# Chunk attention and two feed-forward layers on one core: another block order at the start of the first layer, and one list of single operations for 48 steps

## The chip, the cores and the metric

One NeuronCore of a Trainium2 chip. The metric is the device time of one execution in microseconds; 1665.48 us is the median of three runs of the kernel before.

## The reference

Attention within chunks of 64 positions on float32 q, k and v of shape (8, 8, 576, 64), then a feed-forward layer whose activation is a quotient of two polynomials, then one with the activation s * relu(h)^2 + b. Both layers have 4608 tokens, a model width of 512 and a hidden width of 2048.

```python
scores = scale * np.matmul(q_c, k_c.transpose(0, 1, 2, 4, 3))
scores = scores - np.max(scores, axis=-1, keepdims=True)
attn = np.exp(scores)
attn = attn / (np.sum(attn, axis=-1, keepdims=True) + 1e-09)
out = np.matmul(attn, v_c)
...
h = x @ w_in
P = a[0] + a[1] * h + a[2] * h2 + a[3] * h3
Q = 1.0 + np.abs(b[0]) * np.abs(h) + np.abs(b[1]) * h2
g = P / (Q + 1e-06)
return (g @ w_out).astype(np.float32)
...
h = x @ w_in
r = np.maximum(h, 0.0)
g = s * (r * r) + b
return (g @ w_out).astype(np.float32)
```

## The kernel before

**Tiles and steps.** The 4608 tokens are nine blocks of 512; the hidden width is sixteen slices of 128. A step is one block and one slice: a first product h = w_in x (`mm1`, token M, twelve matmuls of 128x128 by 512 columns), the activation (tokens B, t, r, p, b, l, E, N), a split of its result g into a high and a low part (H, y), and a second product into the block's four accumulators (`mm2`, token R, twelve matmuls). Every operand is held as a high and a low half in a reduced float format, hence three matmuls for each product. The first layer has 144 steps; the second begins in the same manner and goes on with a scheme of seven products for pairs of blocks (`finish`), whose work stays as it is.

**Banks.** h of step i lies in one of three PSUM banks, i modulo 3. The activation writes its exponential back into h and reads it last in `ew_d` (token N, three VectorE operations, the last at line 608). So `mm1` of step i waits for `ew_d` of step i-3.

**Weights.** A slice of w_in or w_out arrives as 512 KB of 64-bit words (token w, `w_stage`, into one of four buffers big0 to big3). ScalarE takes the words apart (f, two operations), VectorE clamps, shifts and joins them for two slices at once (g, lines 396, 400 and twice 403), GpSimd adds (c, line 406), ScalarE makes the high half (d) and GpSimd or VectorE the low half (G or D, line 417). There are 32 such tiles, numbered w0 to w31 in the order in which the steps come to need them.

**Attention.** It runs in 36 groups of 128 rows, four to a block. q and k of each of the first eight groups arrive in four transfers of 64 partitions (P, `att_load_rows`, line 194), which read a chunk of 64 positions from each of two batches; v comes in four (L). These groups use weight buffers of the second half of the slices that are still empty (tags w1_8 to w1_15 and w0_8 to w0_15). TensorE transposes q and k (T), ScalarE copies them out (q, k, line 270), TensorE forms scores (S), VectorE takes the maximum and subtracts it (s, two operations for each of two halves, lines 301 and 302), ScalarE exponentiates (e), VectorE sums and inverts (m, lines 313 to 315), GpSimd or VectorE normalises (n), TensorE transposes (A) and multiplies by v (V); ScalarE writes the high half of the block's x (v) and VectorE the low half (u, line 366). Later groups are turned by VectorE instead (X, line 277). Two buffers hold x of two blocks.

**Order.** Nothing is reordered: each engine runs its instructions in the order in which the program issues them, and the DMA queues of SP and of ACT stand in the order of these two engines' instructions. `START` is a string of tokens, a letter and a number each, that `play` turns into calls: it holds steps 0 to 32, except the tail of the last ones. Its operations are whole ones: g1P is four VectorE operations in a row. A loop of one fixed pattern follows for the steps up to 127, with the attention of later groups laid in by a table of times (`att_at`). The steps' blocks go 0, 1, 0, 1 with half of the slices each, then 2, 3 and on with all sixteen; the first halves' results of blocks 0 and 1 are stored to memory (`store`) and loaded and added (`part_load`, `add`) when the second halves end.

Of the kernel before, what the change touches and what calls it, by code (L numbers as in the profile page):

```python
# [59 lines left out]
)  # L60

BEGUN = 33

# [38 lines left out]
def tile_chunk_attention__then__rational_ffn__then__relu2_ffn(  # L102
# [80 lines left out]
    def heads(n):  # L183
        u, j = divmod(n, S // CH)
        return 2 * H * u, j * CH

    def att_load_rows(n, dma=SP):


        h0, s0 = heads(n)  # L190
# [1249 lines left out]
```

## Time and profile before

| what | value |
|---|---|
| median of three runs (1665.36 to 1665.6) | 1665.48 us |
| the profiled execution: its own time | 1667.5 us |
| the profiled execution: its span of instructions | 1665.4 us |
| PE (TensorE) busy | 1604.4 us, 96% |
| DVE (VectorE) busy | 1311.4 us, 79% |
| ACT (ScalarE) busy | 1091.3 us, 66% |
| POOL (GpSimd) busy | 678.1 us, 41% |

The busy shares are means over the whole span. The page also gives them in 40 slices of 41.6 us, as tenths (9 is 90% or more), with the granted clock of TensorE and the DMA engines' share:

```profile
PE   4689999999999999999999999899999999999997
...
DVE  5899988887788878788789867877457886788677
...
PEclk8899999999999999999999999999999999999999
DMA  9643224112231321313123242897577659666854
```

A reader looks at the left end: the first four or five slices differ from the rest on every row. A row of the timeline gives start and length in us, engine, line, operation, output and inputs, how many, and in square brackets how long the engine stood idle before it and what ended that. "Idle" in the text is a stretch's length less the engine's busy time in it.

### The profile page before, as it was taken

To read this page: it belongs to the slowest core of one execution; us is meant where nothing else is said; L and a number is where in the kernel's file an instruction comes from. 1 tells how busy PE (TensorE), PEld (TensorE's weight loads), DVE (VectorE), ACT (ScalarE), POOL (GpSimd) and SP (SyncE) were. 2 spreads that over 40 slices of the span, in tenths; PEclk is the share of its full clock that TensorE was granted. 3 is DMA by queue.
4 is the path that set the end of the run, shared out by engine and by line. 5 is a ranking of instruction groups with operands and counts; after the bars stand their busy time and mean duration, and the time that the engine had idled before them with its cause. 6 is when DMAs were issued, how large, how long until landed. Compare 5 with 4: busy or idle time off the path is not lost.

```text
span 1665.4 us, 26182 instructions
## 1 busy us (share of the span) xinstructions
PE 1604.4 (96%) x9148; PEld 1313.3 (79%) x9148; DVE 1311.4 (79%) x2071; ACT 1091.3 (66%) x1824; POOL 678.1 (41%) x576
## 2 busy tenths in 40 slices
PE   4689999999999999999999999899999999999997
PEld 3577777888888888888887888788888888888886
DVE  5899988887788878788789867877457886788677
ACT  5778765666666666666687777667565766576563
POOL 4678775666556655666577656210000000000000
PEclk8899999999999999999999999999999999999999
DMA  9643224112231321313123242897577659666854
GB/s 205 160 124 115 73 55 111 34 29 64 39 57 31 60 39 33 59 31 77 33 82 112 92 127 101 276 325 246 190 252 241 194 151 276 219 222 161 286 182 67
DMA packets 339971, 217.76 MB, mean 131 GB/s; under 512 B 262528, under 2 KB 297344, under 8 KB 339840
## 3 DMA queue, kind: packets, MB, share of 16 engines
q1 hardware_dynamic: 326320, 211.63, 44.2%
q10 hardware_dynamic: 13520, 4.46, 1.3%
q8 instruction: 72, 1.18, 0.3%
q14 instruction: 59, 0.48, 0.1%
HBM read 163.58 MB, written 52.43 MB: 130 GB/s over the span
## 4 chain that ended last, share of the span: by engine, by line
PE 85%; DVE 8%; ACT 2%; issue 2%; DMA 1%; POOL 1%; SPq 0%; DVEq 0%; ACTq 0%; POOLq 0%
PE acc L478 27%; PE ae L1041 12%; PE h L460 9%; PE h L461 9%; PE h L462 9%; PE hA L980 8%; PE hE L980 4%; PE hc L980 2%; PE hc L1041 2%; PE pat L350 1%; PE pat L289 1%; PE pat L325 1%; DVE h L607 1%; DVE t L608 1%; DVE ah L606 1%
## 5 line engine op out<-in xcount | busy, mean ns | idle before, releaser
L460 PE MATMUL h<-xh,w 128*128 128x512 f32 x768 | 308.6, 402 | 9.3 <-DVE t L608 5.2
L462 PE MATMUL h<-xh,w 128*128 128x512 f32 x768 | 301.7, 393 | 0.0
L461 PE MATMUL h<-xl,w 128*128 128x512 f32 x768 | 301.5, 393 | 0.0
L478 PE MATMUL acc<-gh,w 128*128 128x512 f32 x1152 | 285.5, 390 | 0.6 <-ACT gh L616 0.6
L478 PEld LDWEIGHTS acc<-gh,w 128*128 128x128 f32 x1152 | 215.7, 188 | 46.0 <-ACT gh L616 1.0
L1041 PE MATMUL ae<-gs,wo 128*128 128x512 f32 x864 | 219.4, 391 | 2.3 <-DVE acc L1062 1.2
L568 POOL TENSOR_SCALAR r<-ah,ab_sb 128x512 f32<-128x512 f32 x138 | 110.1, 798 | 235.4 <-ACT ah L551 235.1
L1041 PEld LDWEIGHTS ae<-gs,wo 128*128 128x128 f32 x864 | 161.8, 188 | 38.6 <-DVE acc L1062 2.4
L571 POOL TENSOR_TENSOR r<-r,ah 128x512 f32<-128x512 f32 x140 | 182.4, 1303 | 13.8 <-ACT r L566 2.2
L460 PEld LDWEIGHTS h<-xh,w 128*128 128x128 f32 x768 | 145.7, 190 | 43.2 <-DVE t L608 8.6
L622 POOL TENSOR_TENSOR gl<-t,gh 128x512 fp32r<-128x512 f32 x129 | 167.8, 1301 | 16.2 <-ACT gh L616 14.5
L462 PEld LDWEIGHTS h<-xh,w 128*128 128x128 f32 x768 | 145.3, 189 | 31.3
L461 PEld LDWEIGHTS h<-xl,w 128*128 128x128 f32 x768 | 145.8, 190 | 29.0 <-DVE xl L366 0.5
L606 DVE SCALAR_TENSOR_TENSOR ah<-r,h 128x512 f32<-128x512 f32 x144 | 98.3, 683 | 79.3 <-ACT h L599 78.7
L478 PE MATMUL acc<-gl,w 128*128 128x512 f32 x576 | 154.2, 390 | 0.0
L980 PE MATMUL hA<-xs,wi 128*128 128x512 f32 x576 | 146.7, 390 | 0.7 <-ACT g L991 0.7
L616 ACT ACTIVATE gh<-t 128x512 fp32r<-128x512 f32 x144 | 90.8, 631 | 78.0 <-DVE t L608 71.4
L406 POOL TENSOR_TENSOR w<-w,wst 128x512 int32<-128x512 int32 x64 | 94.6, 1487 | 79.2 <-DVE w L403 48.5
L980 PEld LDWEIGHTS hA<-xs,wi 128*128 128x128 f32 x576 | 108.0, 188 | 23.7 <-ACT g L991 1.1
L478 PEld LDWEIGHTS acc<-gl,w 128*128 128x128 f32 x576 | 108.1, 188 | 22.6 <-POOL gl L622 0.3
L599 ACT ACTIVATE h<-ah,exb 128x512 f32<-128x512 f32 x144 | 99.5, 691 | 39.1 <-DVE t L590 36.6
L594 ACT ACTIVATE ah<-r,lnb 128x512 f32<-128x512 f32 x144 | 103.4, 718 | 30.3 <-POOL r L571 29.8
(133 smaller groups left out, 3035.2 us busy)
## 6 DMA issues: line engine op xcount, KB each, us to landing
wi<-wq SPq DMA_DIRECT2D x84, 512.0 KB, 4.1
wo<-wq SPq DMA_DIRECT2D x84, 512.0 KB, 4.7
wq<-wo SPq DMA_DIRECT2D x64, 256.0 KB, 3.1
wst<-in_moe_w_out_dram SPq DMA_DIRECT2D x30, 512.0 KB, 4.6
wst<-in_moe_w_in_dram SPq DMA_DIRECT2D x29, 512.0 KB, 5.1
wq<-w SPq DMA_DIRECT2D x48, 256.0 KB, 3.6
qk<-in_q_dram SPq DMA_DIRECT2D x224, 32.0 KB, 2.1
qk<-in_k_dram SPq DMA_DIRECT2D x224, 32.0 KB, 2.1
```

The costliest lines, as they stand in the source:

```text
L460: T.matmul(h, wh, xh[:, kk], start=kk == 0, stop=False)
L461: T.matmul(h, wh, xl[:, kk], start=False, stop=False)
L462: T.matmul(h, wl, xh[:, kk], start=False, stop=kk == KD - 1)
L478: T.matmul(o, l, r, start=first and n == 0, stop=last and n == 2)
L568: eng.tensor_scalar(out=r, in0=ah, scalar1=ab_sb[:, 1:2], scalar2=ab_sb[:, 0:1], op0=ALU.mult, op1=ALU.add)
L571: eng.tensor_tensor(out=r, in0=r, in1=ah, op=ALU.mult)
L594: A.activation(tmp[i]["ah"], tmp[i]["r"], AF.Ln, scale=RS, bias=lnb)
L599: A.activation(h_t[i], tmp[i]["ah"], AF.Exp, scale=-1.0, bias=exb)
L606: V.scalar_tensor_tensor(out=t, in0=r, scalar=ONE, in1=y, op0=ALU.add, op1=ALU.mult)
L622: (eng or (G if i < N1 else V)).tensor_tensor(out=gl, in0=tmp.pop(i)["g"], in1=f(g_t[i][0]), op=ALU.subtract)
L980: T.matmul(ps[b], w[:, l, z * P:(z + 1) * P], x[:, z], start=n == 0 and p in (1, 2, 5), stop=n == 5, skip_group_check=True)
L1041: T.matmul(o, w[:, e, l, dp * P:(dp + 1) * P], gx[t, 2 * u + e, k][0][:, g], start=n == 0 and p in (1, 2, 5), stop=n == 5, skip_group_chec ...
```

## The change

Four things change at once.

1. The blocks of the first 48 steps go 0 and 1 (first halves of the slices), 2 (all slices), 1 and 0 (second halves). Slices 8 to 15 are so needed from step 24 on, not from step 16; block 2's x, groups 8 to 11 of the attention, from step 16 on, not from step 32. Since two buffers hold x, block 0's x is written to memory (`x_out`, token W) and read back (`x_back`, token Y).
2. `START` now holds steps 0 to 47 (`BEGUN` is 48), in another order, and names single operations: g3Pa, g3Pb, g3Pc and g3Pd are the four VectorE operations of one pair of weights, s1a to s1d those of one score output, and likewise m, b and N; other operations can stand between them. The loads of stored parts are tokens J in the list. 16 low halves of weights are made by VectorE (D) and 16 by GpSimd (G), where it was 8 and 24.
3. For the first eight groups a group is 128 neighbouring positions of one batch, so that q and k come in two transfers of 128 partitions, not four of 64; the final store of such rows is one transfer, not two.
4. The names of x's buffers carry a number (xh0, xh1, xl0, xl1) in place of two turns of one name.

```diff
+    "P1 P3 T1x w0A w1A f0 T3b w2 f1 w3 P2A k1 q1 P4 q3 f2 g1Pa k3 S1a g1Pb g1Pc T4c P5A w4 f3 s1b g1Pd T2y s1a s1d "
+    "g3Pa c0 s1c w5 g3Pb q4 w6 c1 x0 P0A g3Pd Q8 e1 g3Pc d0 S3b c2 s3a s3b G0 q2 k2 k4 S4d S2b m1a c3 s3d s3c s4b "
+    "d1 w7A m1b w8 w9 L2 s4d d2 T5y D2 m1c f4 f5 s4a T0y P6 s2b L1 d3 L3 P7A k5 s2a G1 q5 s4c g5Pa n1 g5Pb S5b s2d "
...
-BEGUN = 33
+BEGUN = 48
...
+    x_d = [dram.tile([P, KD, TB], F32, name=f"x_d{z}") for z in range(2)]
...
-    def att_load_rows(n, dma=SP):
...
+    def rows(n, c):
+        if n < NV:
+            u, j = divmod(n, NV // 2)
+            return u, (2 * j + c) * CH
+        h, s0 = heads(n)
+        return h // H + c, s0
...
-        for x in range(2):
-            for c in range(2):
-                dma.dma_start(
-                    out=qk[c * CH:(c + 1) * CH, x].rearrange("t (h d) -> t h d", h=H),
-                    in_=qkv[x][h0 + c * H:h0 + (c + 1) * H, s0:s0 + CH, :].rearrange("h t d -> t h d"),
-                )
...
+    def att_load_rows(n, dma=SP):
+
+
+        u, s0 = rows(n, 0)
+        for x in range(2):
+            dma.dma_start(
+                out=att_new(n)["qk"][:, x].rearrange("t (h d) -> t h d", h=H),
+                in_=qkv[x][u * H:(u + 1) * H, s0:s0 + P, :].rearrange("h t d -> t h d"),
+            )
...
-    def att_S_out(n):
...
+    def att_S_out(n, part="abcd"):
...
+        y = j % 2
         xt[j] = (
-            xp.tile([P, KD, TB], F32R, tag="xh", name="xh"),
-            xp.tile([P, KD, TB], F32R, tag="xl", name="xl"),
+            xp.tile([P, KD, TB], F32R, tag=f"xh{y}", name="xh"),
+            xp.tile([P, KD, TB], F32R, tag=f"xl{y}", name="xl"),
         )
+
+    def x_out(j):
+        for z in range(2):
+            SP.dma_start(out=x_d[z], in_=f(xt[j][z]))
+
+    def x_back(j):
+        x_new(j)
+        for z in range(2):
+            SP.dma_start(out=f(xt[j][z]), in_=x_d[z])
...
-    for j0 in (0, NB):
-        steps += [(j0 + j, y * HF + m, m == 0, m == HF - 1) for y in range(2) for j in range(2) for m in range(HF)]
-        steps += [(j0 + j, m, m == 0, m == MF - 1) for j in range(2, NB) for m in range(MF)]
+    for j, m0, m1 in ((0, 0, HF), (1, 0, HF), (2, 0, MF), (1, HF, MF), (0, HF, MF), *((j, 0, MF) for j in range(3, NB))):
+        steps += [(j, m, m == m0, m == m1 - 1) for m in range(m0, m1)]
+    steps += [(NB + j, y * HF + m, m == 0, m == HF - 1) for y in range(2) for j in range(2) for m in range(HF)]
+    steps += [(NB + j, m, m == 0, m == MF - 1) for j in range(2, NB) for m in range(MF)]
...
+        n = SPB * (jj - NB) + t
+        at = [u * S + s0 for u, s0 in (rows(n, c) for c in range(2))]
+        if at[1] == at[0] + CH:
+            dma.dma_start(out=out[at[0]:at[0] + P, :], in_=o)
+            return
...
-            if i % N1 in (3 * HF - 1, 4 * HF - 1):
-                part_load(steps[i][0])
```

The order tables show what moves. On ScalarE (ACT), whose instructions also carry its DMA queue, the rows from the first weights on, before (w_121 is the pair w0, w1, and w_170 the pair w2, w3; wst_115, wst_117, wst_119 and wst_130 are the raw words of w0 to w3; qk_152 is group 1):

```order
L391 ACTIVATE w_121<-wst_115 128x512
L393 ACTIVATE wst_115<-wst_115 128x512
L391 ACTIVATE w_121<-wst_117 128x512
L393 ACTIVATE wst_117<-wst_117 128x512
L194 DMA qk_152<-in_q_dram 64x8x64 x2
L194 DMA qk_152<-in_k_dram 64x8x64 x2
L391 ACTIVATE w_170<-wst_119 128x512
L393 ACTIVATE wst_119<-wst_119 128x512
L391 ACTIVATE w_170<-wst_130 128x512
L393 ACTIVATE wst_130<-wst_130 128x512
L413 ACTIVATE w0_0_175<-w_121 128x512
L413 ACTIVATE w0_1_177<-w_121 128x512
```

In the changed kernel the rows behind the conversions of w0 and w1 (qk_157 and qk_202 are groups 2 and 5; qk_117 and qk_121 groups 1 and 3, vq their transposed q; wst_151 and wst_155 are w2 and w3):

```order
L235 DMA qk_157<-in_q_dram 128x8x64
L235 DMA qk_157<-in_k_dram 128x8x64
L302 ACTIVATE qk_117<-h_126 128x512
L302 ACTIVATE vq_118<-pat_125 128x512
L302 ACTIVATE vq_122<-pat_142 128x512
L431 ACTIVATE w_168<-wst_151 128x512
L433 ACTIVATE wst_151<-wst_151 128x512
L302 ACTIVATE qk_121<-pat_142 128x512
L235 DMA qk_202<-in_q_dram 128x8x64
L235 DMA qk_202<-in_k_dram 128x8x64
L431 ACTIVATE w_168<-wst_155 128x512
L433 ACTIVATE wst_155<-wst_155 128x512
```

Between the conversions of the first and of the second pair stand now three copies of q and k, and between w2's and w3's a copy and two DMA issues.

On VectorE (DVE), the first operations before (mx_268 and e_269 are a group's score output):

```order
L396 TENSOR_SCALAR w_121<-w_121 128x1024
L400 TENSOR_SCALAR w_121<-w_121 128x1024
L403 SCALAR_TENSOR_TENSOR w_121<-wst_115,w_121 128x512
L403 SCALAR_TENSOR_TENSOR w_121<-wst_117,w_121 128x512
L396 TENSOR_SCALAR w_170<-w_170 128x1024
L400 TENSOR_SCALAR w_170<-w_170 128x1024
L403 SCALAR_TENSOR_TENSOR w_170<-wst_119,w_170 128x512
L403 SCALAR_TENSOR_TENSOR w_170<-wst_130,w_170 128x512
L417 TENSOR_TENSOR w0_0_175<-w_121,w0_0_175 128x512
L301 TENSOR_REDUCE mx_268<-h_244 128x4
L302 TENSOR_TENSOR e_269<-h_244,mx_268 128x4x64
L301 TENSOR_REDUCE mx_268<-pat_243 128x4
```

and in the changed kernel, from the third operation of the pair w0, w1 on (w_139; w_168 is the pair w2, w3; mx_210, e_224 and sm_326 belong to group 1, mx_284 to group 3):

```order
L443 SCALAR_TENSOR_TENSOR w_139<-wst_135,w_139 128x512
L331 TENSOR_REDUCE mx_210<-pat_173 128x4
L443 SCALAR_TENSOR_TENSOR w_139<-wst_137,w_139 128x512
L331 TENSOR_REDUCE mx_210<-pat_173 128x4
L338 TENSOR_TENSOR e_224<-pat_173,mx_210 128x4x64
L436 TENSOR_SCALAR w_168<-w_168 128x1024
L338 TENSOR_TENSOR e_224<-pat_173,mx_210 128x4x64
L440 TENSOR_SCALAR w_168<-w_168 128x1024
L443 SCALAR_TENSOR_TENSOR w_168<-wst_155,w_168 128x512
L443 SCALAR_TENSOR_TENSOR w_168<-wst_151,w_168 128x512
L331 TENSOR_REDUCE mx_284<-pat_266 128x4 x2
L350 TENSOR_REDUCE sm_326<-e_224 128x8
```

Group 1's score output stands now inside the first pair of weights and between it and the second, and group 3's maxima and group 1's softmax sum follow the second pair.

On SP's queue the first transfers before (qk_124 is group 4, wst_130 and wst_132 are w3 and w4, qk_136 is group 0):

```order
L194 DMA qk_124<-in_q_dram 64x8x64 x2
L194 DMA qk_124<-in_k_dram 64x8x64 x2
L383 DMA wst_130<-in_moe_w_out_dram 128x1024
L378 DMA wst_132<-in_moe_w_in_dram 128x4x256
L194 DMA qk_136<-in_q_dram 64x8x64 x2
L194 DMA qk_136<-in_k_dram 64x8x64 x2
```

and in the changed kernel (qk_117 is group 1, qk_121 group 3, qk_163 group 4; wst_151 is w2, wst_155 w3):

```order
L235 DMA qk_117<-in_q_dram 128x8x64
L235 DMA qk_117<-in_k_dram 128x8x64
L235 DMA qk_121<-in_q_dram 128x8x64
L235 DMA qk_121<-in_k_dram 128x8x64
L418 DMA wst_151<-in_moe_w_in_dram 128x4x256
L423 DMA wst_155<-in_moe_w_out_dram 128x1024
L235 DMA qk_163<-in_q_dram 128x8x64
L235 DMA qk_163<-in_k_dram 128x8x64
```

Two groups stand now ahead of the first weights of this queue, each in half as many transfers.

## Rows read from the trace of the kernel before

**Rows 1.** Busy time by stretches: span, length, busy us (count) by engine, clock, DMA, GB/s.
```profile
0.00:22.00 22.00, 5.95 (x48) 4.09 (x48) 7.15 (x11) 9.47 (x16) 8.07 (x11) 1.00 1.05 216
...
0.00:60.00 60.00, 30.24 (x435) 24.38 (x436) 40.14 (x81) 36.78 (x70) 29.53 (x27) 0.84 0.92 200
60.00:174.80 114.80, 101.89 (x603) 81.17 (x601) 107.82 (x163) 87.31 (x151) 87.11 (x69) 0.95 0.43 116
174.80:300.00 125.20, 123.41 (x838) 99.93 (x839) 111.35 (x179) 83.54 (x140) 86.94 (x76) 1.00 0.31 79
300.00:400.00 100.00, 100.00 (x715) 81.99 (x718) 81.92 (x135) 63.23 (x103) 62.14 (x57) 1.00 0.23 45
```

**Rows 2.** Timeline of VectorE and TensorE around the start of step 18.
```profile
174.01 0.75 DVE L608 SCALAR_TENSOR_TENSOR t<-t,a_sb,h 128x512 f32<-128x512 f32 x1
...
174.81 0.50 PE L460 MATMUL h<-xh,w 128*128 128x512 f32 x1 [1.18 <-DVE t L608]
...
177.67 1.98 PE L478 MATMUL acc<-gh,w 128*128 128x512 f32 x8
179.48 1.19 PE L478 MATMUL acc<-gl,w 128*128 128x512 f32 x4
180.51 0.60 PE L325 MATMUL pat<-ident,e 128*128 128x128 f32 x4
180.86 0.47 PE L460 MATMUL h<-xh,w 128*128 128x512 f32 x1
...
183.78 0.70 PE L289 MATMUL pat<-qkT 64*64 64x64 f32 x32
```

**Rows 3.** VectorE's groups by line, 0 to 184.4 us: count, busy, mean ns, idle before.
```profile
L403 DVE SCALAR_TENSOR_TENSOR w<-wst,w 128x512 int32<-128x512 int32 x30 | 20.5, 725 | 0.5
...
L608 DVE SCALAR_TENSOR_TENSOR t<-t,a_sb,h 128x512 f32<-128x512 f32 x18 | 13.5, 748 | 0.6
...
L589 DVE TENSOR_TENSOR t<-t,h 128x512 f32<-128x512 f32 x18 | 12.2, 676 | 2.4 <-ACT t L557 2.4
...
L400 DVE TENSOR_SCALAR w<-w 128x1024 int32<-128x1024 int32 x15 | 11.9, 790 | 0.5
L417 DVE TENSOR_TENSOR w<-w,w 128x512 fp32r<-128x512 f32 x7 | 6.8, 984 | 0.0
L313 DVE TENSOR_REDUCE sm<-e 128x8 f32<-128x512 f32 x9 | 6.1, 673 | 1.3 <-POOL e L319 0.9 <-ACT e L308 0.3
L622 DVE TENSOR_TENSOR gl<-t,gh 128x512 fp32r<-128x512 f32 x6 | 5.6, 938 | 0.0
L302 DVE TENSOR_TENSOR e<-pat,mx 128x256 f32<-128x256 f32 x13 | 5.5, 424 | 0.6 <-PE pat L325 0.2
...
L366 DVE TENSOR_TENSOR xl<-pat,xh 128x256 fp32r<-128x256 f32 x12 | 4.5, 415 | 0.2 <-ACT xh L358 0.2
L314 DVE TENSOR_SCALAR sm<-sm 128x8 f32<-128x8 f32 x9 | 3.3, 367 | 0.3
...
L571 DVE TENSOR_TENSOR r<-r,ah 128x512 f32<-128x512 f32 x2 | 2.8, 1413 | 0.1
L277 DVE STREAM_TRANSPOSE qkT<-qk 128x512 f32<-128x512 f32 x4 | 2.6, 686 | 0.1
L523 DVE COPY o<-acc 128x1024 f32<-128x1024 f32 x2 | 2.4, 1218 | 0.0
L568 DVE TENSOR_SCALAR r<-ah,ab_sb 128x512 f32<-128x512 f32 x2 | 2.2, 1105 | 0.0
```

**Rows 4.** Timeline of the start: first transposes on TensorE, an issue and operations of ScalarE.
```profile
9.86 1.09 PE L266 MATMUL pat<-ident,qk 128*128 128x128 f32 x4 [9.86 <-DMA qk<-in_q_dram]
...
9.23 0.64 ACTq L194 DMA_DIRECT2D qk<-in_q_dram  x1
...
12.15 0.67 ACT L391 ACTIVATE w<-wst 128x512 f32<-128x512 f32 x1 [2.44 <-DMA wst<-in_moe_w_in_dram]
...
20.17 0.62 ACT L270 ACTIVATE qk<-h 128x512 f32<-128x512 f32 x1
```

More of the change, by code (lines that the diff above doesn't have):

```diff
@@ L205, in att_load_rows @@
         }
+        return att[n]
+    def att_load_rows(n, dma=SP):
[5 more added lines that the diff above has]
+            )
     def att_load(n):
@@ L282, in att_S @@
         qT, kT = st["qT"], st["kT"]
-        ps = st["ps"] = banks or [*map(att_banks(where), range(2))]
+        ps = st["sc"] = banks or [*map(att_banks(where), range(2))]
         for p in range(NP):
@@ L308, in att_exp, with att_sum @@
         A.activation(ef, ef, AF.Exp, scale=scale)
-    def att_sum(n):
-        eh = att[n]["e"].rearrange("t p e k -> t (p e) k")
-        sm = att[n]["sm"] = ap_.tile([P, H], F32, tag="sm", name="sm", bufs=2)
-        V.tensor_reduce(out=sm, in_=eh, axis=AX.X, op=ALU.add)
-        V.tensor_scalar(out=sm, in0=sm, scalar1=1e-9, scalar2=None, op0=ALU.add)
-        V.reciprocal(out=sm, in_=sm)
+    def att_sum(n, part="abc"):
+        for x in part or "abc":
+            if x == "a":
+                sm = att[n]["sm"] = ap_.tile([P, H], F32, tag="sm", name="sm", bufs=2)
+                V.tensor_reduce(out=sm, in_=att[n]["e"].rearrange("t p e k -> t (p e) k"), axis=AX.X, op=ALU.add)
+            sm = att[n]["sm"]
+            if x == "b":
+                V.tensor_scalar(out=sm, in0=sm, scalar1=1e-9, scalar2=None, op0=ALU.add)
+            if x == "c":
+                V.reciprocal(out=sm, in_=sm)
     def att_norm(n, eng=G):
@@ L353, in att_V_hi @@
         j, u = divmod(n, SPB)
-        if u == 0:
+        if j not in xt:
             x_new(j)
@@ L497, in out_store @@
     def out_store(jj, t, o, dma=SP):
[L499 to L501 removed]
+        n = SPB * (jj - NB) + t
[3 more added lines that the diff above has]
+            return
+        for c, row in enumerate(at):
             (SP, dma)[c].dma_start(out=out[row:row + CH, :], in_=o[c * CH:(c + 1) * CH, :])
@@ L583, in ew_a, with ew_b @@
             tmp[i]["g"] = r
-    def ew_b(i):
+    def ew_b(i, part="ab"):
         if i < N1:
             h, t1 = h_t[i], tmp[i]["t1"]
-            V.tensor_tensor(out=t1, in0=t1, in1=h, op=ALU.mult)
-            V.scalar_tensor_tensor(out=t1, in0=t1, scalar=a_sb[:, 1:2], in1=h, op0=ALU.add, op1=ALU.mult)
+            for x in part or "ab":
+                if x == "a":
+                    V.tensor_tensor(out=t1, in0=t1, in1=h, op=ALU.mult)
+                else:
+                    V.scalar_tensor_tensor(out=t1, in0=t1, scalar=a_sb[:, 1:2], in1=h, op0=ALU.add, op1=ALU.mult)
     def ew_ln(i):
@@ L921, in x_load @@
             if "raw" not in hold:
-                hold["raw"] = [xp.tile([P, KD, N], F32, tag=tag, name="raw") for tag in ("xh", "xl")]
+                hold["raw"] = [xp.tile([P, KD, N], F32, tag=tag, name="raw") for tag in ("xh0", "xl0")]
             r0, r1 = hold["raw"]
@@ L1053, in out_add @@
             if "acc" not in hold:
-                hold["acc"] = [xp.tile([P, KD, N], F32, tag=tag, name="acc") for tag in ("xh", "xl")]
+                hold["acc"] = [xp.tile([P, KD, N], F32, tag=tag, name="acc") for tag in ("xh1", "xl1")]
             y, z = where[ORDER[k]]
@@ L1290, in w_mid @@
         def w_mid(n, x=""):
-            ns = (n - 1, n) if x == "P" else (n,)
-            w = pairs[n - 1].rearrange("p z f -> p (z f)") if x == "P" else words[n][4]
-            if x != "C":
-                w_clamp(None, w)
-            w_shift(w)
-            for n in ns:
-                w_top(*words[n][3:])
+            ns = (n - 1, n) if x[:1] == "P" else (n,)
+            w = pairs[n - 1].rearrange("p z f -> p (z f)") if x[:1] == "P" else words[n][4]
+            for y in x[1:] or "abcd"[:2 + len(ns)]:
+                if y == "a":
+                    w_clamp(None, w)
+                elif y == "b":
+                    w_shift(w)
+                else:
+                    w_top(*words[ns["cd".index(y)]][3:])
         def w_add(n, x=""):
```

69 lines of the change are left out of this document (39 added, 30 removed), and 70 rows, old and new, of the table START.

## The prediction

> **What bounds the kernel now.** I read the busy time by stretches first. After 300 us TensorE never idles (100.00 busy in 100 us), and before that it idles 29.8 us in the first 60, 12.9 in the next 114.8 and 1.8 in the 125.2 after those [rows 1]. The change touches the first 48 steps and leaves the number of TensorE's instructions as it is. So the end of the kernel moves by just what those 44.5 us of idleness change by; nothing behind them can gain.
>
> Who causes that idleness shows in the second view, the timeline around step 18. Step 18's first matmul waits 1.18 us for VectorE's line 608 and starts at 174.81, while that instruction, the last operation of step 15, ran from 174.01 for 0.75 us [rows 2]. This is the rule of the three banks for h: step i can start when step i-3's last VectorE operation has read its bank. At that moment VectorE is the bound, so step 18's start is VectorE's work up to there (147.96 us: 40.14 + 107.82) plus VectorE's own idle time: 19.9 us up to 60 us, 7.0 from there to 174.8, together 26.84 [rows 1]. Hence the form of my sum: what the change adds to VectorE's work ahead of that point, less what it adds to TensorE's work ahead of it (that much is not missing later), plus the change of VectorE's idle time. The remaining 1.8 us of TensorE's idleness come after step 18, so what has to be compared at the end is 26.84 + 1.79 = 28.6 us.
>
> **The change, part by part.**
>
> *Work ahead of step 18.* In the new list the third block's attention is brought ahead of step 18 and some weights go back behind it. Counting in both lists what stands ahead of step 15's last VectorE operation, with the means of [rows 3]: one low half of a weight and two softmax norms more, of the same two-operand shape (3 x 0.98 = +2.9 us); three pairs of transposes more (3 x 2 x 0.69 = +4.1); 2.25 pairs of weights fewer, each two wide and two narrower operations (2.25 x 3.03 = -6.8); three softmax sums more (3 x 1.2, the third operation taken as no longer than the second, = +3.7); two denominators fewer (2 x 2.5 = -5.0); three score outputs more (3 x 4 x 0.42 = +5.0); four low halves of x more (4 x 2 x 0.41 = +3.3); four low halves of g fewer (4 x 0.94 = -3.8). Together +3.4 us. The same way of counting gives 154.9 us for all of VectorE's work there, where the window shows 147.96, because neighbours overlap; I scale by 0.955: +3.3 us. TensorE gets ahead of step 18 four transposes of the softmax (0.35 from start to start), three score and four value products (0.70 each) and loses one second product (twelve matmuls at 1.81/8 = 0.227, 2.72) [rows 2]: 1.4 + 4.9 - 2.7 = +3.6 us. The two cancel: -0.3 us, and I take zero. The new block order in itself moves no time; what decides is VectorE's idleness.
>
> *The start.* The first transfers change places. Before, the weights w0, w1 and w2 stand on ACT's queue and group 4's q and k on SP's; now SP's queue begins with the q and k of groups 1 and 3 (0.5 MB each), and w2 and w3 (0.5 MB each) come behind both. The DMA engines are full: share 1.05 and 216 GB/s in the first 22 us, 0.92 and 200 GB/s over 60 [rows 1]. Four 128 KB pieces become two of 256 KB with the same short rows, so I give the merging nothing: it saves a queue some issues (0.64 us for one piece [rows 4]), and the transfers do not wait for the issuing but for the engines. Its bounds: 0, or the two issues saved ahead of the first group's end, 1.3 us.
>
> Bytes then give the times. Before: w2 is reached after 2.1 MB, with 2 us ahead of the first byte 11.7 us, and ScalarE gets it at 12.15 [rows 4], so the reckoning holds. Now: w2 is reached after 2.6 MB if nothing else shares the engines, 14.1 us, or after 3.1 MB when group 2, issued on ACT's queue, shares them, 16.5 us. That queues do share is seen in group 4 before: issued at the very start on SP's queue, its q (0.26 MB) reaches TensorE only at 9.86 us [rows 4], while ACT's queue brought three weight tiles by 12.15. I take 16.5. Behind w2 ScalarE's own order now counts: both conversions of w2 (1.3 us), one copy of k (0.6), two issues for group 5 (2 x 0.64) and the first conversion of w3 (0.66) [rows 4]: VectorE's second pair of weights begins at 20.4 us. By then it has done one pair and most of one score output, 4.1 us with the scale above: 16.3 us idle, where before it had idled 14.9 of the first 22 us [rows 1]. After that the pair and three score operations last to 24.4; the next one in VectorE's new order is group 1's softmax sum, whose exponential stands on ScalarE behind the copy of group 4's q and another two issues. Group 4 lands after 4.7 MB, 23.8 us; four transposes 1.1, copy 0.6, issues 1.3 [rows 4], the exponential, of a copy's shape, 0.6: 27.4 us, a wait of 3.0. Then 1.4 us of work, and the next score maximum, group 4's, needs four more copies (2.1) and the product (0.7, or 0.8 at the granted clock of 0.84) behind the exponential: about 30.3 us, a wait of 1.5. Idle up to there: 20.8 us. From there on each instruction that I followed up to step 0 has its inputs in time. Before, the same count stands at 19.9 at 60 us. Bounds: 16.3 (those two waits vanish) to 24 (w3 lands 3 us later still).
>
> A rule of the Trainium skill speaks against the change here. The Trainium skill, "DMA: Bandwidth & Descriptors", section "Queues, rings and completion order", says that each DMA engine takes turns, packet by packet, between the queues that have work for it; it would put w2 at the later of my two times, and without it the sum would come out 2.4 us lower. The 9.86 us of the first q agrees with it.
>
> *From 60 us to step 18.* Before, 7.0 us idle beside 107.82 us of work, 6.5%. The new list names single operations, so that another one can stand between an operation and its wait. What I can name in the rows is line 589's waiting for ScalarE's numerator t1, 2.4 us in all [rows 3]; in the new list operations on weights and scores stand in front of it. Without it 4.6 us are left, 4.2% of the work. Bounds: 2% and 6.5%.
>
> *From step 18 to step 37.* Here the new order has less air. VectorE's work between step 15's and step 34's end is 19 steps of five operations of 0.68 to 0.75 us (19 x 3.54 = 67, and one step's first two, 1.4), 4.25 pairs of weights (12.9), eight low halves of weights (7.8), twelve of g (11.3), two denominators (5.0), two copies of results (2.4): 108 us, scaled 102 [rows 3]. TensorE's work for 19 steps is 19 x 2 x 2.72 = 103.4 us. So over 19 steps VectorE gains 1.4 us on TensorE. Before, VectorE was busy 111.35 of the 125.2 us behind step 18 [rows 1], gaining over 12 us, so that its further idleness was harmless. Now whatever it idles beyond 1.4 us is late at step 37.
>
> *Traffic of x.* The first block's x goes to memory and back (2 MB each way, some 10 us at 200 GB/s). It goes out after step 0's inputs are there, on SP's queue with weights behind it that are due at step 24; it comes back at step 32 and is needed at step 40, eight steps of 5.44 us later. The DMA engines are busy 0.43 and 0.31 there [rows 1]. I cost it at nothing; if the cover were gone, up to 10 us at step 40. The later result stores of two blocks in one piece instead of two are off every path.
>
> **Sum.** Idle up to step 37: 20.8 + 4.2% of (111 + 102) = 29.8, less the 1.4 that VectorE gains: 28.4, against 28.6 before. Change -0.2 us: against the profiled span of 1665.4 us that is 1665.2, and the median of the runs, 1665.48, lies 0.1 above that span: **1665.3 us, no measurable change**.
>
> **Rivals.** *The finer list keeps VectorE fed* (faster): idle share 2% after 60 us, 20.8 + 4.3 - 1.4 = 23.7, 4.9 us less: 1660.6. For it: VectorE has other work for each wait; against it: the start is poorer than before, and nothing in the rows shows VectorE below 6% idle while it is the bound. *No air behind step 18* (slower): the share stays 6.5% as before, 20.8 + 13.9 - 1.4 = 33.3, 4.7 us more: 1670.2. It decides when VectorE has idled more than about 31 us by step 30; for it speaks that before, VectorE was never busier than 94% over a long stretch. *The change does not do what it says*, the transfers land no sooner for being fewer: that is already in my sum, and gives 1665.3 as well. The opposite, a start that idles only 16.3 us, gives 1660.8 and goes with the faster case.
>
> **How the numbers follow.** A measurement of this kernel can tell about 0.2%, 3.3 us, from no change. Forecast and the third rival, within 3.3 us: 0.48. Faster: 0.29, since both a better start and a better list lead there. Slower: 0.23. The range that leaves some 2 in 10 out reaches past both rivals' times a little: 1659.0 to 1671.0.
>
> **What would show it.** In the changed profile: the second pair of weights on VectorE at 20 to 21 us and about 21 us of VectorE idleness by 60 us (under 18 or over 24 would prove my start wrong); step 0 at 60 us or later, not 56.8; VectorE busy over 95% between 60 and 280 us; TensorE's short waits for the last operation of step i-3 (line 608 before) going on to step 40. Wrong would be a wait of TensorE for x's return, or TensorE idle anywhere behind 320 us.

## The result: 0.5% slower, and the profile after

The changed kernel took 1674.47 us (median of four runs, 1673.83 to 1674.72) beside 1665.42 us for the kernel before: ratio 1.0054, interval 1.0037 to 1.0071. In a second comparison, on another chip, it was 1.0039 (1.0027 to 1.0052), 1674.83 beside 1667.94 us. My 1665.3 us and my range (to 1671.0) were wrong. The kernel went the way of my second rival, no air behind step 18, and past it, in part by terms that no rival had. ("Air" is the time that VectorE gains on TensorE over a stretch.)

Busy time by stretches, columns as in [rows 1], cut where step 18 and step 42 begin in the changed kernel and where step 53 does, from which on both kernels run the same loop:

```profile
0.00:22.00 22.00, 9.93 (x88) 7.55 (x91) 6.78 (x14) 8.71 (x14) 4.10 (x9) 1.00 1.06 254
0.00:60.00 60.00, 29.35 (x437) 23.72 (x437) 39.81 (x81) 35.59 (x68) 24.85 (x24) 0.89 0.92 210
60.00:177.20 117.20, 104.90 (x829) 82.05 (x829) 108.93 (x184) 93.00 (x165) 83.80 (x67) 0.97 0.49 127
177.20:318.10 140.90, 137.13 (x679) 109.36 (x680) 124.99 (x189) 95.27 (x156) 73.91 (x60) 1.00 0.20 56
318.10:395.40 77.30, 74.61 (x562) 59.63 (x561) 61.58 (x105) 45.49 (x77) 46.40 (x40) 1.00 0.43 110
```

VectorE idles 20.2 us by 60 us (before 19.9) and 8.3 from there to step 18 (before 7.0). Step 18 starts at 177.18 instead of 174.81 [rows 2], with more of TensorE's work already done: 134.2 us of it up to there, 132.1 before. So up to there the change costs little. But in [rows 1] TensorE was idle 1.8 us behind step 18; now it is idle 3.8 us up to step 42 and 2.7 us from there to step 53. What TensorE waits for between steps 18 and 53 (in all, times, longest), the kernel before from 174.8 to 388.3 us, the changed one from 177.2 to 395.4:

```profile
PE h L460 <- DVE t L608: 1.2, 1, 1.2
PE h L289 <- DVE t L608: 1.2, 1, 1.2
PE acc L478 <- ACT gh L616: 0.6, 1, 0.6
```

The changed kernel:

```profile
PE h L511 <- DVE t L671: 3.8, 8, 1.1
PE acc L529 <- DVE xl L406: 1.0, 1, 1.0
PE pat L390 <- ACT eT L375: 0.7, 1, 0.7
PE pat L365 <- POOL e L359: 0.4, 2, 0.2
PE acc L529 <- ACT gh L679: 0.3, 1, 0.3
```

(The first wait of each list is step 18's own, or includes it.) The eight waits of line 511 are first products waiting for the last operation of step i-3 (line 671, line 608 before): the banks' rule, now eight times. The next two are one place, 343 to 347 us, where the list ends.

Where TensorE's granted clock is 1.00 throughout, the stretch from step 18 to step 53 repeats to a tenth of a microsecond, so most of what follows goes by it. Step 0's matmuls ran at either of the clock's two levels. The order of the last part is planned when the kernel is built and differs from build to build (VectorE's and ScalarE's instructions stand in another order in the two traces of one and the same kernel); step 53 to the end took 1275.3 to 1281.4 us. Two comparisons of one kernel can therefore differ by some 2 us. From the traces (us):

| kernel | VectorE idle by 60 us | step 18 starts | step 18 to 53 | TensorE idle in it | ratio to before |
|---|---|---|---|---|---|
| before, its second trace | 19.9, 19.0 | 174.8, 173.8 | 213.5, 213.5 | 1.8, 1.7 | 1 |
| changed, its second trace | 20.2, 19.7 | 177.2, 175.9 | 218.3, 218.2 | 6.5, 6.4 | 1.0054, 1.0039 |
| b_merge, b_merge2 | 16.7, 17.2 | 172.0, 172.1 | 213.5, 213.5 | 1.8, 1.8 | 0.9979, 0.9976 |
| b_first | 15.7 | 169.9 | 213.5 | 1.7 | 0.9971 |
| b_noclamp | 22.7 | 169.0 | 215.3 | 2.3 | 0.9976 |
| a_split | 27.9 | 184.7 | 218.2 | 6.4 | 1.0086 |
| a_start | 21.5 | 181.7 | 219.9 | 6.3 | 1.0050 |
| a_whole | 27.4 | 201.2 | 229.1 | 14.1 | 1.0231 |
| a_noclamp | 23.6 | 172.6 | 215.3 | 4.4 | 0.9995 |
| a_nop | 19.0 | 176.2 | 218.9 | 7.1 | 1.0035 |
| a_ypool | 19.2 | 177.8 | 222.6 | 8.7 | 1.0084 |
| a_tail2 | 19.5 | 176.7 | 216.6 | 4.9 | 1.0062 |
| a_both | 19.8 | 177.1 | 219.4 | 7.3 | 1.0048 |
| a_more | 19.6 | 176.6 | 221.7 | 3.7 | one run |

Four of these rows hold something that no edit put there. In b_noclamp, a_start and a_ypool TensorE's granted clock fell to 0.50 for 3.4 us between steps 18 and 53, in a_whole twice. In the lines below, busy time as above, the granted clock stands third from the end; the first two are of b_noclamp (behind a wait of TensorE of 1.7 us) and a_ypool (behind the waits at the list's end), the third is of a_start:

```profile
216.12:219.53 3.41, 3.41 (x9) 2.65 (x9) 3.24 (x8) 1.94 (x3) 2.94 (x3) 0.50 0.02 5
350.09:353.50 3.41, 3.41 (x10) 2.63 (x9) 0.00 (x0) 1.04 (x2) 1.69 (x2) 0.50 0.44 68
351.03:354.44 3.41, 3.41 (x9) 2.63 (x9) 0.00 (x0) 1.26 (x2) 1.91 (x2) 0.50 0.43 66
```

Steps 42 to 48 took 49.0 us in a_ypool and in a_start, and 47.3 in the changed kernel, with the same 2.3 us of idleness: such a fall costs some 1.7 us. Each kernel was traced once or twice, so that nothing here ties the falls to the edits.

### The profile page after: what moved, and what is told of

The parts are those of the page before. It is cut to its first block, busy times and chain, and to the rows that moved or that the text cites. A ratio compares the mean times of both kernels' runs of the same rounds, so it can differ in the third digit from the quotient of the medians.

```text
span 1672.7 us, 26145 instructions
## 1 busy us (share of the span) xinstructions
PE 1606.3 (96%) x9148; PEld 1310.0 (78%) x9148; DVE 1314.6 (79%) x2088; ACT 1097.7 (66%) x1836; POOL 648.0 (39%) x547
## 4 chain that ended last, share of the span: by engine, by line
PE 78%; DVE 9%; DMA 3%; ACT 3%; issue 2%; POOL 2%; SPq 1%; DVEq 0%; ACTq 0%; POOLq 0%
PE acc L529 25%; PE ae L1104 11%; PE h L511 8%; PE h L513 8%; PE h L512 8%; PE hA L1043 8%; PE hE L1043 4%; PE hc L1043 2%; PE hc L1104 2%; DMA qk<-in_q_dram 2%; DVE h L669 1%; SPq L251 1%; DVE ah L667 1%; PE pat L390 1%; DVE t L645 1%
## 5 line engine op out<-in xcount | busy, mean ns | idle before, releaser
L529 PEld LDWEIGHTS acc<-gh,w 128*128 128x128 f32 x1152 | 214.7, 188 | 47.1 <-issue 1.4
L1104 PE MATMUL ae<-gs,wo 128*128 128x512 f32 x864 | 219.4, 391 | 1.9 <-DVE acc L1125 1.2
L622 POOL TENSOR_SCALAR r<-ah,ab_sb 128x512 f32<-128x512 f32 x127 | 104.2, 821 | 224.1 <-ACT ah L605 224.0
L685 POOL TENSOR_TENSOR gl<-t,gh 128x512 fp32r<-128x512 f32 x120 | 157.8, 1315 | 26.9 <-ACT gh L679 13.8
L611 ACT ACTIVATE t<-h,a_sb 128x512 f32<-128x512 f32 x144 | 111.3, 773 | 17.5 <-DVE gl L685 6.0
```

Of the source, the lines that this page charges most:

```text
L529: T.matmul(o, l, r, start=first and n == 0, stop=last and n == 2)
L611: A.activation(t1, h_t[i], AF.Identity, scale=a_sb[:, 3:4], bias=a_sb[:, 2:3])
L622: eng.tensor_scalar(out=r, in0=ah, scalar1=ab_sb[:, 1:2], scalar2=ab_sb[:, 0:1], op0=ALU.mult, op1=ALU.add)
L685: (eng or (G if i < N1 else V)).tensor_tensor(out=gl, in0=tmp.pop(i)["g"], in1=f(g_t[i][0]), op=ALU.subtract)
L1104: T.matmul(o, w[:, e, l, dp * P:(dp + 1) * P], gx[t, 2 * u + e, k][0][:, g], start=n == 0 and p in (1, 2, 5), stop=n == 5, skip_group_chec ...
```

## The experiments

Names with b_ start from the kernel before, names with a_ from the changed one.

**The transfers.** b_merge (and b_merge2, the same kernel again) takes only the merging into the kernel before, with the groups' other rows and the final store that go with it; a_split cuts the transfers of q and k alone in two again in the changed one (in short form):

```diff
-            for c in range(2): dma(qk[c*CH:(c+1)*CH, x] <- 64 positions, 8 heads)
+            dma(qk[:, x] <- 128 positions, 8 heads)          # a_split: the reverse
```

> The kernel before, with only the q and k (and the rows that v and the results take) of the first eight groups moved in the changed kernel's fewer, 128-partition transfers; order, blocks and list stay. Theory A (my prediction: the transfers wait for the engines, not for the issuing): within 1.3 us of the kernel before, 1664 to 1667 us. Rival B (the fewer transfers land differently and are part of the 9 us lost): 2 us or more slower, with VectorE idle for more than 21 us by 60 us.

> The changed kernel with each transfer of q and k of the first eight groups cut back into two of 64 partitions, as many as before the change; the rest stays. Theory A (a transfer over 128 partitions passes faster, as the same step alone in the kernel before showed: 2.3 us of span, 4 us of median): 2.3 to 4.5 us slower than the changed kernel, a ratio of 1.0068 to 1.008 to the kernel before, VectorE's idleness by 60 us 23 us or more instead of 20.2. So the merging hides that the rest of the change costs 11 to 13 us. Rival B (my prediction: transfers wait for the engines whatever their form): within 0.8 us of the changed kernel, ratio 1.005 to 1.006.

> The kernel before with the merged transfers alone once more, beside the other order of them: a ratio of 0.997 to 0.9988 again; if it lies above 0.9995 the first measurement of its gain does not hold.

b_merge fits neither theory: it is faster, by 0.2% twice, with step 18 at 172.0. a_split fits theory A and goes past its bounds, with step 18 7.5 us later. So the merging is no part of the loss; it hides more of it. The queues over the first 24 us (packets, MB, share of the 16 engines' time), in the kernel before:

```profile
q1 hardware_dynamic: 6322, 2.45, 56.0%
q10 hardware_dynamic: 3840, 2.62, 51.0%
```

In b_merge:

```profile
q1 hardware_dynamic: 7290, 2.71, 48.8%
q10 hardware_dynamic: 3808, 2.62, 36.9%
```

5.07 MB took 107.0% before and 5.34 MB take 85.7% with the merging: 24% less engine time per MB. q10 holds four weight tiles and group 1's q and k. The weights, whose transfers did not change, gain as well: their packets of 1 and 4 KB took 36.3% before and take 27.0%, for the same 2.10 MB. TensorE's first transpose in b_merge:

```profile
6.12 1.09 PE L276 MATMUL pat<-ident,qk 128*128 128x128 f32 x4 [6.12 <-DMA qk<-in_q_dram]
```

In [rows 4] the same q, from the same place in the queue, was there at 9.86. The Trainium skill states the rule that I did not weigh: "SBUF — State Buffer", section "Door 1: The DMA port swizzle", says that a transfer over partitions 0 to 63 reaches only half of SBUF's ports. The direction agrees; the runs do not show the ports, and they do not tell the span of a transfer from the number of transfers, since both edits change the two together.

b_first asks what the start waits for once the transfers are merged:

```diff
-w0A w1A w2A f0 P4 w3 w4 f1 P0 T4y ...
+w0A w1 w2A f0 w3 P4 f1 w4 P0 T4y ...
```

> The kernel before with the merged transfers and another order of the first ones: w1 on SP's queue beside w0 on ACT's, w3 ahead of group 4's q and k, whose copies stand behind the first four weights on ScalarE anyway. Theory A (with the transfers merged, the first pair of weights, 10.7 us, is what VectorE waits for): first pair on VectorE at 7.5 to 8.5 us, VectorE's idleness by 60 us 14 to 15 us instead of 16.7, step 18 some 2 us earlier than the 172.0 of the merged kernel, ratio to the kernel before 0.996 to 0.997. Rival B (group 4's q and k, then later, are waited for instead): ratio 0.9975 to 0.9985, as with the merging alone.

Close to theory A. The first pair reaches VectorE at 8.55 us instead of 10.66, VectorE idles 15.7 us by 60 us, and step 18 starts 2.2 us earlier than in b_merge. The ratio, 0.9971 (0.996 to 0.9983), lies just outside either theory's bounds. Its median, 1663.15 us, is the lowest here, but its interval overlaps that of b_merge2 (0.9967 to 0.9985), so the gain of this order over the merging alone is seen in the trace and not clear of noise in the times. a_start tries the same in the changed kernel:

```diff
-P1 P3 T1x w0A w1A f0 T3b w2 f1 w3 P2A ...
+P1 w0A w1A w2A w3 P3 T1x f0 T3b f1 P2A ...
```

> The changed kernel with another order of the first transfers: the weights w0, w1 and w2 first on ACT's queue, w3 on SP's queue behind group 1's q and k and ahead of group 3's; everything behind stays. Theory A (the second pair of weights, reaching VectorE at 18.1 us, is the loss of the start): second pair at 13 to 15.5 us, VectorE's idleness by 60 us 17 to 18 us, step 18 some 2.5 us earlier and the total 2 to 3.5 us shorter than the changed kernel, ratio 1.0035 to 1.0042. Rival B (group 3's q and k, then later, are waited for just as long): the second pair earlier, but the idleness by 60 us 19.5 us or more and the time the same within 0.8 us.

Rival B. VectorE's timeline at the start (us, duration, line, idle before):

```profile
16.90 0.42 DVE L331 TENSOR_REDUCE mx<-pat 128x4 f32<-128x256 f32 x1 [4.69 <-PE pat L321]
...
18.56 1.34 DVE L436 TENSOR_SCALAR w<-w 128x1024 f32<-128x1024 f32 x1
...
35.31 1.28 DVE L350 TENSOR_REDUCE sm<-e 128x8 f32<-128x512 f32 x2 [3.01 <-ACT e L344]
```

The second pair cannot use its earlier weights (18.56 us, 18.09 in the changed kernel). In VectorE's fixed order group 1's score maximum stands ahead of it, whose scores stand on TensorE behind the transposes of group 3's q, and these started at 13.45 us after a wait of 3.8 us for that q. ScalarE's conversions of w2 and w3 stand behind the copies of group 3's q and k and come at 16.30 and 17.88 us. The profile's late step 18 (181.7 us) is not the edit's alone: TensorE ran at the lower clock for 19.9 us between steps 0 and 18, in the changed kernel for 6.8. In a_tail, whose list is the changed kernel's up to there, it was 19.9 us as well, and step 18 started at 179.9.

**Why TensorE waits behind step 18.** Two kernels leave the clamp of the weights out, so their weights are not clamped:

```diff
-    w_clamp(None, w)          # one VectorE operation on each pair, first layer only
```

> The changed kernel without the first of the operations on each pair of the first feed-forward's weights (the clamp to the range of a normal number): 16 VectorE operations of 0.76 us fewer, 12 of them (9.1 us) ahead of step 18, and 2.3 to 3 us of them between steps 18 and 30. Nothing else changes. Theory A (VectorE's volume is the bound up to step 18 and, with no air, up to step 37): 10 to 13 us faster than the changed kernel, 1661 to 1664 us, and TensorE's waits for the last operation of step i-3 gone behind 180 us. Rival B (VectorE mostly waits in its order for ScalarE's and GpSimd's results, so that its volume matters half): 4 to 6 us faster, 1668 to 1670, with those waits still there.

> The kernel before without the clamp of the first feed-forward's pairs of weights: 16 VectorE operations fewer, 14 of them (11.3 us) ahead of step 18. Theory A (VectorE's volume is the bound up to step 18): 9 to 11 us faster than the kernel before, 1654.5 to 1656.5 us. Rival B (waits in the order decide half of it): 4 to 6 us faster, 1659.5 to 1661.5. Beside the same cut in the changed kernel: if that gains 2 us more there than here, lack of VectorE time behind step 18 was part of the loss; if both gain the same, it was not.

The changed kernel goes from 1.0039 (or 1.0054, in the first comparison) to 0.9995, 7.3 or 9.8 us, between the two theories; the kernel before goes to 0.9976, 4 us, rival B. Step 18 comes 4.6 and 5.8 us earlier, half of the work removed. Behind it only the changed kernel gains: 218.3 to 215.3 us. The kernel before loses 1.8 us of its gain again; 0.5 of that is a longer wait for line 608, and behind that wait, at 216 us, the clock fell, so that a second product took 4.5 us instead of 2.9. So VectorE's time is short behind step 18 in the changed kernel and not in the kernel before. a_ypool moves such work to GpSimd instead:

```diff
-y17D y19D y20D y23D ... y38D      (14 low halves on VectorE)
+y17  y19  y20  y23  ... y38       (the same on GpSimd)
```

> The changed kernel with the low halves of g of 14 steps between 17 and 38 on GpSimd (1.3 us each, and it is 56% busy there) instead of VectorE (0.7 to 0.9 us each, some 11 us in all). Theory A (VectorE has no air behind step 18): TensorE's idleness from step 18 to 42 falls from 3.8 us to under 2, the total 1.5 to 3 us faster than the changed kernel. Rival B (waits in the order for ScalarE's and GpSimd's results are the cause, and GpSimd gets later): the same or up to 3 us slower.

Rival B: 4.4 us worse from step 18 to 53, of which 1.7 is the fall of the clock and 2.7 lies between steps 18 and 42, where TensorE now idles 6.0 us. VectorE is busy 90.9 of 105.2 us between steps 18 and 36 there, 93.9 of 103.9 in the changed kernel: less work, more waiting. In that stretch ScalarE waited 10.6 us for GpSimd's low halves and denominators (6.4 in the changed kernel), and VectorE 12.3 us for ScalarE (8.2). That the one makes the other is read from the order, not tried. a_nop gives GpSimd the first half of eight denominators:

```diff
-p13 r13h ... p45 r45h
+r13      ... r45
```

> The changed kernel with the first half of eight denominators (steps 13, 21, 23, 31, 36, 38, 40 and 45) on GpSimd again instead of ScalarE (0.77 us there against 0.80). Theory A (ScalarE's in-order chain is what VectorE's operations wait for behind step 18): 0.5 to 2 us faster. Rival B (GpSimd is the slower of the two there): 0.5 to 2 us slower. Theory C (neither is tight; VectorE's volume and the order of the list are): the same within 0.5 us.

Within 0.7 us between steps 18 and 53, on rival B's side; the ratio (1.0035 beside 1.0039) shows no difference. Whether VectorE lacks air or a step's own chain is too long was left to a_more, which gives TensorE more work there:

```diff
+            if kk == 0 and 18 <= i < 36:
+                T.matmul(h, wh, xh[:, kk], start=True, stop=True)   # twice
```

> The changed kernel with two more products (repeats of the first of the twelve, overwritten by it) at the head of each first product of steps 18 to 35: 36 products, 36 x 0.227 = 8.2 us more TensorE work just where TensorE waits for VectorE, 3.8 us between steps 18 and 42. From step 18 to step 53 the changed kernel takes 218.2 us. Theory A (VectorE has no air there because the attention's TensorE work was moved ahead; more TensorE work gives it air): TensorE's idleness from step 18 to 42 falls under 1.5 us, and step 18 to 53 takes 223.5 to 225 us, 2 to 3 us less than the work added. Rival B (the waits come from the length of a step's own chain through ScalarE and GpSimd, which starts later by the added products too): the idleness stays at 3 us or more, 226 to 227 us.

Theory A, more strongly than it said: 8.2 us of work cost 3.5 us (218.2 to 221.7). The waits on the banks are all but gone (TensorE's waits from 176.6 to 398.3 us; the first includes step 18's own 0.4):

```profile
PE h L512 <- DVE t L674: 1.0, 2, 0.6
PE acc L532 <- DVE xl L406: 1.0, 1, 1.0
PE pat L390 <- ACT eT L375: 0.7, 1, 0.7
```

More was saved than the 2.7 us of idleness that went. A first product that has waited takes longer: summed over its twelve matmuls 3.02 us, against 2.76 for one that joins the work before it (means over steps 18 to 52 of the changed kernel; 3.02 and 2.78 before). Ten of the 35 waited, four in a_more, one before. So each wait costs 0.25 us more, which counts as busy; I call it a refill.

**The end of the list.** VectorE's timeline there, in the changed kernel:

```profile
343.30 0.76 DVE L338 TENSOR_TENSOR e<-pat,mx 128x256 f32<-128x256 f32 x2 [0.98 <-PE pat L365]
343.97 1.28 DVE L584 TENSOR_TENSOR o<-o 128x512 f32<-128x512 f32 x2
345.40 0.76 DVE L406 TENSOR_TENSOR xl<-pat,xh 128x256 fp32r<-128x256 f32 x2
```

TensorE's:

```profile
343.95 0.69 PE L390 MATMUL pat<-eT,vs 64*64 64x64 f32 x32 [0.69 <-ACT eT L375]
344.57 0.73 PE L529 MATMUL acc<-gh,w 128*128 128x512 f32 x2
346.30 0.93 PE L529 MATMUL acc<-gh,w 128*128 128x512 f32 x3 [0.99 <-DVE xl L406]
```

Between two blocks' sums groups 13 to 15 borrow the accumulators' banks. Step 40's second product has to wait until line 406 has copied group 14 out, and on VectorE that stands behind an addition (line 584) that nothing waits for here. a_tail tried another order and was mis-made: it put group 14's transposes ahead of its softmax's normalisation in the program, so that its output lacks that, and TensorE waited 6 us at one place. It says nothing on the theory of this place. a_tail2 is the mended order, a_both is that and a_ypool's edit together.

```diff
-V13b ... n14 ... S15a ... M47 ... A14y ... X16 ... u13 ... V14b v14 s15c R40 s15d Z39 ... u14
+a_tail:  A14y V13b ... n14 ... S15a ... M47 ... a14 v13 ... u13 V14b v14 ... R40 ... u14 X16 Z39
+a_tail2: V13b ... n14 ... A14y S15a ... v13 a14 ... u13 V14b M47 ... v14 s15c s15d ... u14 R40 X16 Z39
```

> The changed kernel with the end of its list in another order: group 14's four transposes go ahead of group 13's value product and of step 47's first product, the copies, and the VectorE work that step 40's second product waits for, go ahead of group 16's transposes and of the addition of the half results. Theory A (the place where the list ends costs 2.2 us of TensorE idleness between 340 and 366 us, because of attention that stands in the accumulators' banks): 1.5 to 2.5 us faster than the changed kernel, about 1672.3 us, and that idleness under 0.8 us. Rival B (what is saved there is lost again at once, since VectorE or ScalarE is late in any case): same time as the changed kernel within 0.7 us, 1673.8 to 1675.2, with the idleness moved behind 350 us.

> The changed kernel with the end of the list mended: group 14's transposes stand ahead of group 15's scores, its value product ahead of step 47's first product, and what step 40's second product waits for (two copies out of the accumulators' banks) ahead of group 16's transposes and the addition of the half results. Theory A (TensorE's waits between 339 and 347 us, 1.86 us, come from this order): 1 to 1.9 us faster than the changed kernel, TensorE's idleness from step 42 to 48 at most 1.3 us instead of 2.3. Rival B (VectorE or ScalarE is late in any case): the same time, the idleness moved.

> Both edits together, the other end of the list and the low halves on GpSimd. Theory A: the two gains add up, 2.5 to 5 us faster than the changed kernel, with TensorE's idleness from step 18 to 53 under 4 us instead of 6.5. Rival B: no more than the better of the two.

In a_tail2 step 42 to 48 takes 45.6 us instead of 47.3, TensorE idle 0.9 instead of 2.3: theory A for the place. Its median is no better (1.0062; its last part, from step 53 on, took 1280.2 us), so for the whole kernel it is undecided. In a_both each part does what it did alone, 6.0 us of idleness from step 18 to 42 as in a_ypool and 45.7 us from step 42 to 48 as in a_tail2, so it lies between them: rival B.

**Single operations.** a_whole puts groups of operations together again:

```diff
-g11Pa ... g11Pb ... g11Pc ... g11Pd      N0a ... N0b ... N0c
+                              g11P                       N0
```

> The changed kernel with the single operations of a score output, a softmax sum, a weight pair, a product of the numerator and an end of a step put together again, each group where its last operation stood. Theory A (single operations let VectorE fill its waits; the loss has other causes): 2 to 6 us slower than the changed kernel, with more of VectorE's idleness between 60 and 180 us. Rival B (the fine order itself interferes: operations of one group stand apart, other engines get their results later): faster than the changed kernel by 1 us or more.

Slower, as theory A has it, and far beyond its bound: 33 us between the medians (in the trace, of 34.8 us at step 53, up to 3.4 are falls of the clock). This list was made for single operations, so it does not tell what a list made for whole ones would do; between 60 us and step 18 VectorE waits 8.3 us for copies of x alone:

```profile
DVE xl L393 <- ACT xh L385: 8.3, 4, 5.1
DVE ah L654 <- ACT h L643: 4.9, 4, 2.9
```

**Step 0's clock.** Second traces of both kernels:

> The changed kernel itself, on the chip of the other runs, so that they have their own base and a second trace. Theory A (the 2 us by which the profiled execution of the kernel before was longer than its timed runs lie in step 0, whose twelve products ran at half the clock, 0.449 us each, where the changed kernel's took 0.270): where step 0 runs at half the clock in this trace too, its span is 2 to 4 us longer than the 1672.7 us of the first one, and TensorE's idleness from step 18 to 53 is 6.4 us again. Rival B: the spread has another place in the program.

> The kernel before itself, for a second trace of it. Theory A (2 us of its first trace lie in step 0 at half the clock): where step 0's products stand closer than 0.449 us here, step 18 starts up to 2 us earlier than 174.8; from step 18 to 53 it takes 213.5 us again. Rival B: step 18 is as late whatever step 0's clock.

Busy time while step 0 runs, with the granted clock third from the end, in the first trace of the kernel before:

```profile
56.83:59.80 2.97, 2.97 (x6) 2.09 (x7) 2.94 (x6) 2.84 (x5) 1.10 (x2) 0.50 0.37 102
```

In the first trace of the changed one:

```profile
59.95:62.90 2.95, 2.85 (x11) 2.14 (x12) 2.45 (x6) 1.86 (x5) 0.89 (x1) 1.00 0.85 291
```

0.50 is 1.2 GHz, 1.00 is 2.4 GHz. A matmul of step 0 took 0.449 us in the first trace of before, 0.402 in the second (step 18 then 1.0 us earlier), 0.270 and 0.373 in the two of the changed kernel. Theory A for before; for the changed kernel the second trace, with the slower step 0, is not longer at step 18 but 1.3 us shorter, so step 0's clock alone does not decide there. Where the clock was low for longer it does reach step 18: a_tail has the same list up to there, and step 0 wholly at the lower clock,

```profile
59.65:65.20 5.55, 5.55 (x12) 3.72 (x12) 3.77 (x8) 0.96 (x3) 2.29 (x2) 0.50 0.29 107
```

and, with 19.9 us at that clock from there to step 18 in all, step 18 started at 179.9 us. So the 2 us by which the first profile of before exceeds its timed runs may lie partly in step 0; the rest is not settled. The profiles differ by 7.1 us at step 53 (6.8 in the second traces), the medians by 9.05 and 6.9.

## Why the prediction was wrong, step by step

- **Work ahead of step 18** (cancels): held. My form of the sum gave 147.96 + 3.3 + 25.5 = 176.8 us for step 18; it started at 177.18. But the parts were off: VectorE's work is +0.8 us, not +3.3, and its idleness from 60 us on 8.3 us, not 4.7 (7.6% of the work, outside my 2 to 6.5%). Two errors cancelled, so the right sum was luck. Of the 8.3 us, the waits of the numerator's product for ScalarE (line 645, 589 before) were 1.4, less, as I had thought; but 1.7 are one wait for a transfer of k (line 309) that I did not have.
- **The start** (20.8 us idle): 20.2, as forecast, for a wrong reason. I gave the merging nothing; a_split shows 27.9 without it. My sum of bytes had 216 GB/s, and it was 254 in the first 22 us; the second pair came at 18.1 us, not 20.4, and the rest was waited for later. The term "0, at most 1.3 us" for the merging failed: step 18 comes 1.7 to 2.8 us earlier by it in the old order, 7.5 in the new one. That the transfers wait for the engines fits the runs, but it hid that the engines' time for the same bytes depends on how the transfers are cut. Nor does the 9.86 us of the first q speak for queues taking turns, the rule that I cited from the Trainium skill ("DMA: Bandwidth & Descriptors", "Queues, rings and completion order"): with the same neighbours it is 6.1 us when merged. No run here tests that rule.
- **Steps 18 to 37** (1.4 us of air): the mechanism was right, two terms of it were mis-sized, and the stretch cost more than I had. My terms gave 103.4 us of TensorE's work and 2.9 of idleness, 106.3 us; it took 109.4, TensorE busy 106.0 and VectorE 98.5. VectorE's work was less than my 102 (and 108 us times my 0.955 is 103, a slip that hid that only 0.3 us of air were left by my own count). Its idleness was far more, 10.9 us, 11% of its work, where I had 4.2%. Busy time between steps 18 and 36 in the kernel before:

```profile
174.81:287.34 112.53, 111.34 (x784) 90.26 (x785) 101.39 (x163) 74.53 (x126) 78.40 (x67) 1.00 0.31 76
```

In the changed one:

```profile
177.18:281.11 103.93, 100.60 (x432) 80.49 (x433) 93.89 (x134) 71.73 (x117) 58.47 (x47) 1.00 0.21 67
```

VectorE is idle a tenth of either stretch, 11.1 and 10.0 us, waiting in its order, in the changed kernel mostly for ScalarE (from 177.2 us on, these three are its longest waits):

```profile
DVE ah L667 <- ACT h L656: 3.3, 4, 1.1
DVE t L645 <- ACT t L611: 1.9, 3, 1.3
DVE t L645 <- ACT ah L605: 1.8, 2, 1.3
```

Before, TensorE had 111.3 us of work there, 10 more than VectorE, and did not notice. With the attention moved ahead it has 100.6, 6.7 more than VectorE: the 3.3 us that are missing are its idleness. I took VectorE's idleness of before behind step 18 for slack that would go away when needed; it was the cost of in-order waits, and stayed. To this come the refills (nine or ten waits more at 0.25 us, most of them here), a term that my sum did not have. Of my signs, "VectorE busy over 95% between 60 and 280 us" failed with 92%, and its 35.2 us of idleness by step 30 are past the 31 that I had set for the rival. By the rival's 6.5% this stretch would have had 6.6 - 1.4 = 5.2 us of loss; it had 3.3 of idleness, and TensorE's work was 2.6 us more than my 103.4, most of it refills.
- **Behind step 37** (nothing): failed. I gave the list's end no cost and had not read where R40 stands in the new order; it costs 2.7 us of TensorE idleness from step 42 on, and a_tail2 takes 1.5 of them away. My sign "TensorE idle anywhere behind 320 us" showed it.
- **Traffic of x** (nothing): held as far as the trace shows, no wait for it appears; it was not tested by itself. Nor does any run have the new order of the blocks with another list, so what the block order costs by itself stays open.

Together, from step 18 to 53: I expected 213.5 - 1.8 - 3.6 + 2.9 = 211.0 us, and it took 218.25. Of the 7.2 us, 3.6 are idleness (2.7 at the list's end, 0.9 before it), 2.4 products that took longer, mostly by refills (1.6 in first products, 0.8 in second ones), and the last 1.3 the moved attention, whose matmuls behind step 18 fell by 5.05 us where I had reckoned 6.3. So two terms failed above all: the list's end, which I had put at nothing without a reason, and the price of a wait beyond its idleness, which the sum lacked. VectorE's in-order waits were priced at 4.2% of its work where they were 11%, and that error was partly hidden by its work being less than I had reckoned. By step 53 the profiles account for 7.1 and 6.8 us of the medians' 9.05 and 6.9; the 2 us left in the first comparison are not settled.

## What to carry to other kernels

Read the idle share of the engine that will become the bound from the very stretch in which it will be the bound: an engine that waits in order for others can be full at 90% busy, as VectorE was here, and work moved away from its partner takes away its cover. Try the larger transfers, here over all 128 partitions, before changing any order: that edit alone gained 0.2%, and the whole change lost 0.4 to 0.5%. Before a difference of 2 us is put down to an edit, look whether the clock was the same in both traces. Where a hand-made order ends and borrowed banks are handed back, follow each wait to the instruction that stands needlessly ahead.

## What the runs showed of the hardware

A VectorE operation can take more than twice its time while GpSimd runs an operation on two tensors. VectorE's line 443, two at a time, in the changed kernel, first with GpSimd idle and then beside it:

```profile
19.75 1.29 DVE L443 SCALAR_TENSOR_TENSOR w<-wst,w 128x512 int32<-128x512 int32 x2
...
70.75 2.37 DVE L443 SCALAR_TENSOR_TENSOR w<-wst,w 128x512 int32<-128x512 int32 x2
```

GpSimd's timeline in the second place:

```profile
71.09 1.48 POOL L625 TENSOR_TENSOR r<-r,ah 128x512 f32<-128x512 f32 x1 [2.54 <-ACT r L620]
72.53 1.73 POOL L457 TENSOR_TENSOR w<-w,w 128x512 fp32r<-128x512 f32 x1
```

In the whole trace line 443's operations take 0.68 to 0.69 us each with GpSimd idle and 0.68 to 1.82 beside such an operation. Over the kernel it is busy 54.6 us where the same 64 operations (line 403) took 47.1 before, and it overlaps GpSimd's operations on two tensors for 17.2 us where it was 11.5. That this is the cause was read from the traces, not tried.
